# Moving the result transposes, the PSUM banks and the weight conversions in an attention + two-MLP kernel

## The chip, the cores and the metric

The kernel runs on one core of a Trainium2 chip. The metric is the device time of one execution in microseconds (us). Lower is better.

The core has a matrix engine (TensorE; PE in the profile, PEld its weight loads), a vector engine (VectorE; DVE), a scalar or activation engine (ScalarE; ACT), GpSimd (POOL) and a queue engine that here only issues transfers (SyncE; SP). Each runs its instructions in their order in its own stream, and waits on semaphores for the others. PSUM, the memory that TensorE writes to, has eight banks, and a bank holds one 128 x 512 float tile.

## The reference, cut to what matters

```python
k_all = concat([k_g, k_l]); v_all = concat([v_g, v_l])
out_g = softmax(scale * q_g @ k_all.T) @ v_all          # 32 global queries per head see all 544 keys
s_ll = where(|i - j| <= 32, scale * q_l @ k_l.T, -1e9)  # 512 local queries per head see a band
s_lg = scale * q_l @ k_g.T                              # and the 32 global keys
out_l = softmax(concat([s_lg, s_ll])) @ v_all
x = concat([out_g, out_l]) as (2176, 512) tokens        # 4 batches, 8 heads, head size 64
h = x @ w_in;  x2 = max(0.01 * h, h) @ w_out            # 512 -> 2048 -> 512
h = x2 @ w_in2;  out = (h - tanh(h)) @ w_out2           # 512 -> 2048 -> 512
```

The four weight matrices come as 64-bit floats; all else is 32-bit. The MLP products are each made as three products of split operands (high x high, low x high, high x low).

## The kernel before, in words

**Attention stages.** `stage(s)` (L889) holds one pair of heads and one half (256 queries) of a batch: 32 stages, two halves to a pair of heads, eight stages to a batch. A stage is a list of operations that the caller puts between other work:

- `keys` (odd stages): `k_prep` and `q_prep` transpose the next pair's keys and queries through PSUM, and `k_glob` adds the global keys.
- the scores: `score` (L452) makes 32 small products into two banks (`sps`), `smax_a` (L471) takes the minimum and the exponentials. From stage 10 on, four DVE instructions add the mask, reduce, and are the only readers of the two score banks.
- `cols` (L895): `av(s - 2)` multiplies the probabilities of two stages earlier by the values into a bank `avps`, and DVE divides by the sums (`av_out`, tile `o`); `g_score(s)` makes the global queries' scores into the same bank; `copy_v` has POOL rearrange values (`vx`). `g_run` calls what is due of the global part: `g_min`, `g_exp`, `g_norm`, `g_trans` (five transposes into the banks of tags `gtps` and `gt2ps`), `g_av` (40 products into `gavps`), and then `load_v`.
- `turns` (L947): `p_trans(s - 1)` (L495) transposes the probabilities of the stage before (`ptps`, copied out by ACT as `pt`).

`o_trans(pp, tag)` (L537) transposes a stage's result `o` into a bank `otps`; ACT copies it out rounded (`xh`), and DVE subtracts that from the bank (`xl`): the two halves of the MLP's input. Only after `xl` is the bank free. In stages 3 to 9 `o_trans(s - 3)` stands in `turns`; stage 9 has a second one, of stage 7's result, into the bank of tag `avps`. From stage 11 on it is called by `score_op` (L930), right before the scores of stage s:

```python
if s > PRE and s - 1 not in ends:
    o_trans(s - 3, tag("otps"))
score(s, [tag("sps0"), tag("sps1")])
smax_a(s)
```

and `score_op` and `cols` are one operation there (L942).

**Banks.** In stages 0 to 9 each kind of tile has a bank of its own (`start_tags`, L874). Afterwards the attention has three (`run_tags`, L878), given out in turn by `tag` (L882): a tile takes the bank of the third request before it. The bank `h` and the four banks `y0` to `y3` belong to the MLPs by then.

**MLP items.** An item (phase, c, f) is block f of 16 of the hidden layer for a chunk c of tokens (`sizes`: 512, 512, 512, 256 and 384). `mlp1_a` makes twelve matmuls into the bank `h` in four steps, and ACT's activation `g` empties it; `mlp1_b`, two items later, makes twelve into the y banks in four steps. The order of items (L1058) makes stretches: items 0 to 7 are chunk 0 with the first half of f, 8 to 23 chunk 1, 24 to 31 chunk 0 with the second half of f, 32 to 47 chunk 2, 48 to 63 chunk 3, 64 to 79 chunk 4; then the second MLP. Stages 0 to 9 run ahead of item 0; stages 10 to 17 are spread between the steps of items 0 to 7, 18 to 25 between those of items 24 to 31, and the rest beside items 32 to 47 (`beside`, L1065 to L1079). Each such run of stages ends with the transpose of its last result.

**Conversions.** A weight block of 64-bit floats (512 KB) is loaded into one of two buffers (`wraw`, issued by SP) and converted: `rebias` on ACT, then `first`, `second`, `third` on DVE (`convert_parts`, L140); after `third` the buffer is free, and `job` (L828) issues the load of the job after next into it. Blocks of the first output matrix are then split into `woh` and `wol`, used and stored; blocks of the second MLP's matrices (`w2f`) are only stored, for later. `job_at[n]` (L989 to L1009) says how many jobs run beside item n: the first at its start, a second at its middle. Before: items 1 to 8, 11 to 13, 15 and 16 one each, 17 to 22 two each, 23 and 24 one, 35 to 47 one or two (17 jobs), 49, 51, 53 and 55 one. `y_part` (L252) loads a partial sum back into the same two buffers, at items 27 and 29; it is added at the end of item 33.

**What sets the order.** PE's order up to item 77 is the program's (`manual_schedule`, L978 to L984). Those of ACT, DVE and SP are the program's until stage 9 is through (`InTurn`, L21); after that a scheduler places them by its own timeline. `behind` keeps conversions back behind the latest attention and MLP instructions issued by then.

Of the kernel before, what the change touches and what calls it, by code (L numbers as in the profile page):

```python
# [37 lines left out]
def kernel(  # L38
# [28 lines left out]
    PRE, SKEW = 10, 2  # L67
# [174 lines left out]
    HF = NF // 2  # L242
# [189 lines left out]
    def k_glob(j):  # L432
        b, p = divmod(j, NP)
        to = k_t[j][:, :640].rearrange("p (k n) -> p k n", k=5)
        vector.tensor_copy(to[:, :, 96:], kgt[b % 2][:, p : p + 1].to_broadcast([128, 5, SG]))
# [433 lines left out]
    def g_run(n):  # L869
# [3 lines left out]

    start_tags = {  # L874
        "kps": "h", "qps": "att0", "sps0": "att1", "sps1": "y0", "avps": "att2", "sgps": "y1", "ptps": "y2", "otps": "y3",
        "qgps": "h", "gavps": "att2", "gtps": "att0", "gt2ps": "h",
    }
    run_tags = ["att0", "att1", "att2"]  # L878
    ntag = [0]
# [2 lines left out]
    def tag(kind):  # L882
        if tags[0] is start_tags:
            return start_tags[kind]
        t = tags[0][ntag[0] % len(tags[0])]
        ntag[0] += 1
        return t

    def stage(s):  # L889


        ops, late = [], []
        last = NU // 2 - 1

        def cols():  # L895
            ps = bank(tag("avps"), "avps")
            outs = []
            if s >= 2:
                outs.append(av(s - 2, ps))
            if s <= last:  # L900
                outs.append(g_score(s, ps[:, 4 * (D + 1) :] if s >= PRE else bank(tag("sgps"), "sgps")))
            if s < PRE:
                late.append(outs.pop())
            for o in outs:
                o()
            if s >= 1:
                copy_v(s - 1)
            if s <= last and s % 4 == 3:
                j = s // 2
                b, quad = j // NP, j % NP // 2  # L910
                gtodo.extend([
                    (2 * s + 1, lambda: g_min(b, quad)),
                    (2 * s + 2, lambda: g_exp(b, quad)),
                    (2 * s + 3, lambda: g_norm(b, quad)),
                    (2 * s + 5, lambda: g_trans(b, quad, [tag("gtps"), tag("gt2ps")])),
                    (2 * s + 7, lambda: (g_av(b, quad, tag("gavps")), load_v(2 * b + quad + 2))),
                ])
                gtodo.sort(key=lambda x: x[0])
            g_run(2 * s)

        def keys():
            j = (s + 1) // 2
            k_prep(j, tag("kps"))
            k_glob(j)
            q_prep(j, tag("qps"))
            load_kq(j + 2)

        if s % 2 and s + 1 <= last:
            ops.append(keys)
        def score_op():  # L930
            if s > PRE and s - 1 not in ends:
                o_trans(s - 3, tag("otps"))
            score(s, [tag("sps0"), tag("sps1")])
            smax_a(s)

        if s <= last:
            ops.append(score_op)
        else:
            ops.append(lambda: s - 1 in ends or o_trans(s - 3, tag("otps")))
        ops.append(cols)  # L940
        if s >= PRE and s <= last:
            cols_op, first_op = ops.pop(), ops.pop()  # L942
            ops.append(lambda: (first_op(), cols_op()))

        def turns():  # L947
            if 1 <= s <= last + 1:
                p_trans(s - 1, tag("ptps"))
            if 3 <= s < PRE:  # L950
                o_trans(s - 3, tag("otps"))
            if s == PRE - 1:
                o_trans(s - 2, tag("avps"))
            while late:
                late.pop()()
            if s % (2 * NP) == 3 and s // (2 * NP) + 1 < B:
                qg_prep(s // (2 * NP) + 1, tag("qgps"))
            g_run(2 * s + 1)
            if s % (2 * NP) == 1 and s // (2 * NP) + 1 < B:
                qg_load(s // (2 * NP) + 1)  # L960

        ops.append(turns)
        return ops

    ends = (17, 25)
# [23 lines left out]
    job_at, due = {}, 0.0  # L989
# [2 lines left out]
    REST = 2 * NF + 2  # L992
    for n in range(4 * NF - 3):
        out_f = 1 <= n <= HF or 2 * HF < n <= 3 * HF
        early = 11 <= n < 23 and n != 14
        if n > REST:
            due += 7.2 if n < 3 * NF else 2.9
        job_at[n] = int(out_f) + int(early) + int(due / 5.5)
        due %= 5.5
        if out_f:  # L1000
            jobs.append(("out", w1_out, o_todo.pop(0)))
        for _ in range(job_at[n] - int(out_f)):
            if w2_todo:
                jobs.append(w2_todo.pop(0))
            else:
                job_at[n] -= 1
        if n == 3 * HF:
            jobs.extend([None] * 2)
    assert not w2_todo and not o_todo  # L1009

    if True:
# [10 lines left out]
        load_v(0)  # L1022
        in_load()
        k_prep(0, tag("kps"))
        q_prep(0, tag("qps"))
        qg_prep(0, tag("qgps"))
        k_glob(0)
        load_kq(2)
        parts, lows = [], []
        for pp in range(PRE):  # L1030
# [36 lines left out]
        for last, n0, n1 in ((17, 0, HF), (25, 3 * HF, 4 * HF), (NU // 2 + 1, 2 * NF, 3 * NF)):  # L1067
            ops = []
# [28 lines left out]
        for n in range(len(items) + 8):  # L1097
            ph, c, f = items[n] if n < len(items) else (3, 0, 0)
            one = items[n - 1] if 0 < n <= len(items) else (3, 0, 0)
            if ph == 1:  # L1100
                if n in (0, 2, 4, 6) or HF <= n < 2 * HF:
                    in_job()
                if n in (0, 2, 3) or 4 <= n < 12:
                    with tc.issue_after(last_kq[0].ins):
                        in_load()
                if n == REST:
                    job_load()
                    job_load()
                jobs_now = job_at.get(n, 0)
                if jobs_now:  # L1110
                    job()
                if n in (3 * HF + 3, 3 * HF + 5):
                    y_part((n - 3 * HF - 3) // 2)
                if c == 4 and f == 0:
                    while gtodo:
                        gtodo.pop(0)[1]()
                    assert not raws and not jobs
                    att_ctx.close()
                    p2 = ctx.enter_context(tc.tile_pool(name="p2", bufs=1))
                    for k in range(NF - 1):  # L1120
                        wo2_t.append([p2.tile([128, ND, 128], F32R, name=f"wo2{x}{k}") for x in "hl"])
                    wo2_t.append([x[0][:, :, 512:] for x in (xh, xl)])
                    x2_load(0, 0)
                    x2_load(0, 1)
                if c == 4:
                    w2_fetched = [fetch2(w2o_dram[f], False), fetch2(w2i_dram[f], f >= 3 + ND)]
                    if 3 <= f < 3 + ND:
                        x2_split(0, f - 3)
            elif ph == 2 and order2.index(c) + 1 < 5:
                nx = order2[order2.index(c) + 1]  # L1130
                if f in (2, 3):
                    x2_load(nx, f - 2)
                if 5 <= f < 5 + ND:
                    x2_split(nx, f - 5)
            if n in fetch_at:
                fetches.extend(items1[m][2] for m in fetch_at[n])
            while fetches:
                wo_fetch(fetches.pop(0))
            ops = beside.pop(n, [])
            if ph == 2:  # L1140
                mlp2_a(c, f)
            if ph == 3:
                while p_t:
                    mlp2_split()
            steps, last = [], []
            for k in b_at.get(n, []):
                p, c1, f1 = items[k]
                if p == 1:
                    steps += mlp1_b(c1, f1)
                else:  # L1150
                    last.append((c1, f1))
            if ph == 1:
                steps = mlp1_a(c, f) + steps
            if ph == 1 and not ops and gtodo:
                ops = [gtodo.pop(0)[1]]
            K, M = len(ops), len(steps)
            at = [int((i + 0.5) * M / K) for i in range(K)]
            for m, step in enumerate(steps):
                if ph == 1 and jobs_now > 1 and m == M // 2:
                    job()  # L1160
                step()
                while at and at[0] <= m:
                    at.pop(0)
                    ops.pop(0)()
            for op in ops:
                op()
            for c1, f1 in last:
                mlp2_b(c1, f1)
            if ph == 1 and c == 4:
                for kind, t in zip(("out", "in"), w2_fetched):  # L1170
                    behind(lambda: w2_place(kind, f, t))
            fix(n + 1)
            stores()
# [30 lines left out]
```

## Time and profile before

| | |
|---|---|
| median of 3 runs | 917.63 us (916.68 to 918.47) |
| the profiled execution | 917.32 us, of which the span of its instructions is 915.4 us |
| PE busy | 877.8 us (96% of the span) |
| DVE busy | 612.1 us (67%) |
| ACT busy | 505.3 us (55%) |
| POOL busy | 124.2 us (14%) |
| chain that ended last | PE 83%, DVE 7%, DMA 4%, ACT 4% |

Times in the profile are microseconds from the first instruction. "A <- B" behind a wait says that B ended it. A name such as `avps` is a tile, L72 the helper that issues all matmuls, L30 the helper through which ACT, DVE and SP are called. PEclk is the clock that TensorE was granted, as a share of 2.4 GHz; it has two levels, 1.0 and 0.5, so a mean between them tells for what part of a stretch it was at the lower. Busy times of a pipelined engine overlap, so a group of matmuls is best read by its first start and the next group's.

### The profile page before, as it was taken

How to read it: one execution, taken by the hardware profiler on the slowest of the kernel's cores; microseconds unless marked ns; L12 is line 12 of the kernel's file. 1: busy time of each engine (PE TensorE's matmuls, PEld its weight loads, DVE VectorE, ACT ScalarE, POOL GpSimd, SP SyncE). 2: the span in 40 equal slices, each digit the busy share in tenths (PEclk: the TensorE clock that was granted, in tenths of full speed). 3: DMA queues.
4: the chain of work that ended last, by engine and by line, in shares of the span. 5: the costliest groups of instructions: out<-in, count | busy, mean ns of one | idle time of the engine just before them, and what ended most of it. 6: DMA issues, size and time to landing. Idle time of an engine off the chain costs nothing.

```text
span 915.4 us, 18283 instructions
## 1 busy us (share of the span) xinstructions
PE 877.8 (96%) x6908; PEld 743.6 (81%) x6908; DVE 612.1 (67%) x1363; ACT 505.3 (55%) x1053; POOL 124.2 (14%) x247
## 2 busy tenths in 40 slices
PE   7889899998999999999999999999999999999998
PEld 5667778886777877789999998888888888899997
DVE  4667767766624356554323468888878888888886
ACT  5767665444655355434334566565556555655564
POOL 5654420000423132100000000000000000000022
PEclk9989999999999999999999999999999999999999
DMA  9658779678655476679966752001000100010010
GB/s 202 151 151 244 209 217 270 206 221 247 204 135 133 120 219 202 206 227 298 328 202 198 245 196 81 1 18 63 1 1 24 46 1 1 1 47 1 0 36 23
DMA packets 120167, 123.08 MB, mean 134 GB/s; under 512 B 62736, under 2 KB 82448, under 8 KB 120080
## 3 DMA queue, kind: packets, MB, share of 16 engines
q1 hardware_dynamic: 117552, 121.21, 44.2%
q10 hardware_dynamic: 2528, 0.72, 0.4%
q8 instruction: 54, 0.88, 0.4%
q14 instruction: 33, 0.27, 0.1%
HBM read 95.16 MB, written 26.74 MB: 133 GB/s over the span
## 4 chain that ended last, share of the span: by engine, by line
PE 83%; DVE 7%; DMA 4%; ACT 4%; issue 1%; ACTq 0%; SPq 0%; DVEq 0%
PE h L72 38%; PE o L72 20%; PE y L72 17%; DMA wraw<-in_moe_w_out_dram 3%; PE avps L72 2%; DVE wt L30 2%; PE gavps L72 1%; DVE wf L30 1%; DVE xl L30 1%; PE ptps L499 1%; ACT e L30 1%; DVE gl L30 1%; PE qps L441 1%; DMA yraw<-yd 1%; PE sps L72 1%
## 5 line engine op out<-in xcount | busy, mean ns | idle before, releaser
L72 PE MATMUL h<-xh,win 128*128 128x512 f32 (+2 forms) x1280 | 356.4, 362 | 6.2 <-ACT g L30 5.3
L72 PEld LDWEIGHTS h<-xh,win 128*128 128x128 f32 x1280 | 231.5, 190 | 41.5 <-ACT g L30 7.2
L72 PE MATMUL h<-xl,win 128*128 128x512 f32 (+2 forms) x640 | 230.4, 360 | 0.0
L391 POOL COPY vx<-vr 32x260 f32<-32x260 f32 (+3 forms) x208 | 101.1, 486 | 260.1 <-issue 142.9
L72 PEld LDWEIGHTS h<-xl,win 128*128 128x128 f32 x640 | 121.5, 190 | 15.6
L30 DVE TENSOR_TENSOR gl<-g,gh 128x512 fp32r<-128x512 f32 (+2 forms) x80 | 50.0, 626 | 119.8 <-ACT gh L30 119.6
L72 PE MATMUL y<-gh,woh 128*128 128x512 f32 (+2 forms) x320 | 118.8, 371 | 0.0
L72 PE MATMUL y<-gh,wol 128*128 128x512 f32 (+2 forms) x320 | 114.7, 358 | 1.0 <-DMA wol<-wod 1.0
L72 PE MATMUL y<-gl,woh 128*128 128x512 f32 (+2 forms) x320 | 114.3, 359 | 0.0
L72 PE MATMUL o<-wo2l,gh 128*128 128x512 f32 x255 | 99.6, 391 | 0.0
L72 PE MATMUL o<-wo2h,gh 128*128 128x512 f32 x255 | 99.4, 390 | 0.0
L72 PE MATMUL o<-wo2h,gl 128*128 128x512 f32 x255 | 97.4, 390 | 0.0
L30 ACT ACTIVATE g<-h 128x512 f32<-128x512 f32 (+2 forms) x80 | 42.6, 533 | 97.7 <-PE h L72 97.0
L30 ACT ACTIVATE u<-h 128x512 f32<-128x512 f32 (+2 forms) x80 | 42.6, 533 | 89.0 <-PE h L72 81.3
L721 POOL TENSOR_TENSOR gl<-p,gh 128x256 fp32r<-128x256 f32 x16 | 11.8, 740 | 518.8 <-ACT gh L30 516.9
L30 ACT ACTIVATE gh<-p 128x512 fp32r<-128x512 f32 (+2 forms) x80 | 45.5, 568 | 41.9 <-DVE p L30 41.8
L72 PEld LDWEIGHTS y<-gh,woh 128*128 128x128 f32 x320 | 60.5, 189 | 8.0
L72 PEld LDWEIGHTS y<-gl,woh 128*128 128x128 f32 x320 | 60.3, 188 | 8.0
L72 PEld LDWEIGHTS y<-gh,wol 128*128 128x128 f32 x320 | 60.6, 189 | 7.6 <-DMA wol<-wod 1.4
L30 ACT ACTIVATE u<-u,consts 128x512 f32<-128x512 f32 (+2 forms) x80 | 52.7, 658 | 6.8 <-DVE p L30 4.1
L721 DVE TENSOR_TENSOR gl<-p,gh 128x512 fp32r<-128x512 f32 (+1 forms) x64 | 41.9, 654 | 21.4 <-ACT gh L30 21.3
L72 PEld LDWEIGHTS o<-wo2h,gl 128*128 128x128 f32 x255 | 47.9, 188 | 10.1
(116 smaller groups left out, 1361.1 us busy)
## 6 DMA issues: line engine op xcount, KB each, us to landing
wraw<-in_moe_w_out_dram SPq DMA_DIRECT2D x32, 512.0 KB, 4.7
woh<-wod SPq DMA_DIRECT2D x64, 256.0 KB, 4.1
wol<-wod SPq DMA_DIRECT2D x64, 256.0 KB, 3.4
inraw<-in_moe_w_in_dram SPq DMA_DIRECT2D x16, 512.0 KB, 5.6
wraw<-in_moe_w_in_dram SPq DMA_DIRECT2D x16, 512.0 KB, 5.0
wod<-woh SPq DMA_DIRECT2D x16, 256.0 KB, 4.8
wod<-wol SPq DMA_DIRECT2D x16, 256.0 KB, 4.7
w2id<-w2f SPq DMA_DIRECT2D x16, 256.0 KB, 5.2
```

Source lines behind the costliest of these rows:

```text
L30: got = getattr(self.engine, name)(*args, **kwargs)
L72: nc.tensor.matmul(o, lhsT, rhs, start=start, stop=stop, skip_group_check=shared)
L391: last_cp.append(nc.gpsimd.tensor_copy(to, src))
L441: nc.tensor.transpose(ps[:, 128 * t : 128 * t + 128], qr[:, t].rearrange("p h d -> p (h d)"), ident)
L499: nc.tensor.transpose(ps[:, k * 128 : k * 128 + 128], e[:, k // 2, k % 2], ident)
L721: eng["pool" if i == order2[-1] else "dve"].tensor_sub(gl[:, :N], p, f32(gh)[:, :N])
```

## The change

- From stage 11 on, `o_trans(s - 3)` moves out of the operation that begins with the scores, to `turns`, right behind `p_trans(s - 1)`. It is the same stage's later operation, with MLP steps between. As the requests for banks now come in another order, so do the banks.
- Stage 7's result is transposed in item 0, ahead of its third step (of four), and no longer at the end of stage 9.
- Stages 0 to 9: `gavps` goes to the bank `att0` and not `att2`; `gt2ps` to `y2` (that of `ptps`) and not `h`; the first `g_av`, with the `load_v` behind it, comes one operation later (in `cols` of stage 7, not `turns` of stage 6).
- At the very start `qg_prep(0)` and `k_glob(0)` come ahead of `q_prep(0)`, with the bank of `otps` in place of `h`.
- Conversions: items 17, 19 and 21 have one job and not two; items 25 to 30, which had none, have one each; items 35 to 47 have one each (13 jobs and not 17); then 49, 52, 54, 57 and 59. `y_part` issues both its loads at item 31.

```diff
--- before.py
+++ after.py
@@ -873,7 +873,7 @@
 
     start_tags = {
         "kps": "h", "qps": "att0", "sps0": "att1", "sps1": "y0", "avps": "att2", "sgps": "y1", "ptps": "y2", "otps": "y3",
-        "qgps": "h", "gavps": "att2", "gtps": "att0", "gt2ps": "h",
+        "qgps": "h", "gavps": "att0", "gtps": "att0", "gt2ps": "y2",
     }
     run_tags = ["att0", "att1", "att2"]
     ntag = [0]
@@ -913,7 +913,7 @@
                     (2 * s + 2, lambda: g_exp(b, quad)),
                     (2 * s + 3, lambda: g_norm(b, quad)),
                     (2 * s + 5, lambda: g_trans(b, quad, [tag("gtps"), tag("gt2ps")])),
-                    (2 * s + 7, lambda: (g_av(b, quad, tag("gavps")), load_v(2 * b + quad + 2))),
+                    (2 * s + (7 if s > PRE - 4 else 8), lambda: (g_av(b, quad, tag("gavps")), load_v(2 * b + quad + 2))),
                 ])
                 gtodo.sort(key=lambda x: x[0])
             g_run(2 * s)
@@ -927,20 +927,12 @@
 
         if s % 2 and s + 1 <= last:
             ops.append(keys)
-        def score_op():
-            if s > PRE and s - 1 not in ends:
-                o_trans(s - 3, tag("otps"))
-            score(s, [tag("sps0"), tag("sps1")])
-            smax_a(s)
-
         if s <= last:
-            ops.append(score_op)
-        else:
-            ops.append(lambda: s - 1 in ends or o_trans(s - 3, tag("otps")))
+            ops.append(lambda: (score(s, [tag("sps0"), tag("sps1")]), smax_a(s)))
         ops.append(cols)
         if s >= PRE and s <= last:
-            cols_op, first_op = ops.pop(), ops.pop()
-            ops.append(lambda: (first_op(), cols_op()))
+            cols_op, score_op = ops.pop(), ops.pop()
+            ops.append(lambda: (score_op(), cols_op()))
 
 
 
@@ -949,8 +941,8 @@
                 p_trans(s - 1, tag("ptps"))
             if 3 <= s < PRE:
                 o_trans(s - 3, tag("otps"))
-            if s == PRE - 1:
-                o_trans(s - 2, tag("avps"))
+            if s > PRE and s - 1 not in ends:
+                o_trans(s - 3, tag("otps"))
             while late:
                 late.pop()()
             if s % (2 * NP) == 3 and s // (2 * NP) + 1 < B:
@@ -992,11 +984,11 @@
     REST = 2 * NF + 2
     for n in range(4 * NF - 3):
         out_f = 1 <= n <= HF or 2 * HF < n <= 3 * HF
-        early = 11 <= n < 23 and n != 14
+        early = n in (11, 12, 13, 15, 16, 18, 20, 22) or 3 * HF < n < 4 * HF - 1
         if n > REST:
             due += 7.2 if n < 3 * NF else 2.9
-        job_at[n] = int(out_f) + int(early) + int(due / 5.5)
-        due %= 5.5
+        job_at[n] = int(out_f) + int(early) + int(due / 7.1)
+        due %= 7.1
         if out_f:
             jobs.append(("out", w1_out, o_todo.pop(0)))
         for _ in range(job_at[n] - int(out_f)):
@@ -1004,7 +996,7 @@
                 jobs.append(w2_todo.pop(0))
             else:
                 job_at[n] -= 1
-        if n == 3 * HF:
+        if n == 4 * HF - 2:
             jobs.extend([None] * 2)
     assert not w2_todo and not o_todo
 
@@ -1022,9 +1014,9 @@
         load_v(0)
         in_load()
         k_prep(0, tag("kps"))
+        qg_prep(0, tag("otps"))
+        k_glob(0)
         q_prep(0, tag("qps"))
-        qg_prep(0, tag("qgps"))
-        k_glob(0)
         load_kq(2)
         parts, lows = [], []
         for pp in range(PRE):
@@ -1109,8 +1101,9 @@
                 jobs_now = job_at.get(n, 0)
                 if jobs_now:
                     job()
-                if n in (3 * HF + 3, 3 * HF + 5):
-                    y_part((n - 3 * HF - 3) // 2)
+                if n == 4 * HF - 1:
+                    y_part(0)
+                    y_part(1)
                 if c == 4 and f == 0:
                     while gtodo:
                         gtodo.pop(0)[1]()
@@ -1156,6 +1149,8 @@
             K, M = len(ops), len(steps)
             at = [int((i + 0.5) * M / K) for i in range(K)]
             for m, step in enumerate(steps):
+                if n == 0 and m == 2:
+                    o_trans(PRE - 3, tag("otps"))
                 if ph == 1 and jobs_now > 1 and m == M // 2:
                     job()
                 step()
```

## Rows read from the trace of the kernel before

**Rows 1.** The page: the span, and busy time, share and instructions of each engine.

```profile
span 915.4 us, 18283 instructions
PE 877.8 (96%) x6908; PEld 743.6 (81%) x6908; DVE 612.1 (67%) x1363; ACT 505.3 (55%) x1053; POOL 124.2 (14%) x247
```

**Rows 2.** PE's waits, whole span: what waited, for what; us in total, times, longest.

```profile
PE avps L72 <- DVE xl L30: 12.3, 19, 1.9
...
PE gavps L72 <- DVE o L30: 2.3, 1, 2.3
...
PE otps L542 <- DVE o L30: 1.7, 1, 1.7
...
PE h L72 <- ACT pg L30: 0.8, 1, 0.8
```

**Rows 3.** Stretches: us; busy PE, PEld, DVE, ACT, POOL (instructions); PEclk, DMA share, GB/s.

```profile
36.00:43.00 7.00, 5.65 (x130) 5.12 (x130) 3.40 (x12) 2.90 (x9) 1.21 (x4) 0.76 0.28 64
54.00:63.00 9.00, 8.16 (x98) 5.86 (x96) 5.64 (x19) 4.89 (x14) 3.92 (x9) 0.62 0.34 120
62.00:133.00 71.00, 64.40 (x882) 51.10 (x881) 48.95 (x151) 49.97 (x118) 28.88 (x52) 0.98 0.72 201
115.00:121.00 6.00, 4.99 (x58) 4.00 (x58) 4.09 (x17) 2.77 (x8) 2.75 (x6) 0.72 0.42 134
...
214.00:220.00 6.00, 5.89 (x19) 4.68 (x20) 4.52 (x8) 2.12 (x5) 0.00 (x0) 0.72 0.82 255
238.00:310.00 72.00, 68.58 (x955) 54.84 (x955) 28.69 (x125) 40.53 (x102) 23.57 (x54) 1.00 0.46 128
```

**Rows 4.** Timeline, one stage beside items 0 to 7: start, us, instruction [idle before].

```profile
113.13 0.38 PE L542 MATMUL otps<-ident,o 128*128 128x128 f32 x2
...
113.44 0.67 PE L72 MATMUL sps<-kt,qt 64*32 64x128 f32 x32
...
116.01 0.25 PE L72 MATMUL avps<-vr,pt 128*32 128x65 f32 x2 [1.91 <-DVE xl L30]
...
117.53 0.28 DVE L30 CUSTOM_DVE_ANT_0 e<-sps,mask 128x128 f32<-128x128 f32 x1
```

**Rows 5.** PE's waits from 190 to 330 us, the same columns as in rows 2.

```profile
PE h L72 <- ACT g L30: 4.3, 3, 2.2
```

**Rows 6.** Pieces of the chain that ended last: start, us, what.

```profile
7.73 0.63 PE qgps L564 x4
...
37.35 2.01 PE gavps L72 x40
...
175.81 2.72 PE y L72 x12
...
198.41 0.67 ACT wf L30
...
200.29 0.70 DVE wf L30
...
201.05 3.91 DMA wraw<-in_moe_w_out_dram
...
204.99 0.67 ACT wf L30
```

**Rows 7.** Timeline of ACT behind the first `g_av`.

```profile
39.40 0.22 ACT L30 ACTIVATE xh<-gavps 128x64 fp32r<-128x64 f32 x1 [2.21 <-PE gavps L72]
```

**Rows 8.** Timeline from stage 9 to item 0.

```profile
52.69 0.61 ACT L30 ACTIVATE pt<-ptps 128x512 f32<-128x512 f32 x1
...
53.72 0.41 PE L542 MATMUL otps<-ident,o 128*128 128x128 f32 x2 [1.73 <-DVE o L30]
...
55.51 1.22 PE L72 MATMUL h<-xh,win 128*128 128x512 f32 x2 [0.84 <-ACT pg L30]
```

**Rows 9.** Groups: one POOL copy, 55 to 133 us (first) and 235 to 310: busy, mean ns.

```profile
L391 POOL COPY vx<-vr 32x260 f32<-32x260 f32 x21 | 10.5, 501 | 1.0
...
L391 POOL COPY vx<-vr 32x260 f32<-32x260 f32 x21 | 8.7, 415 | 1.0
```

## The prediction

> **What bounds the kernel now.** First the page: PE is busy for 96% of the span and no other engine for more than 67% [rows 1]. So a gain must come from PE's idle time, or from its clock. Second, PE's waits. The reader should see that one wait outweighs the rest: `avps` waits 19 times for `xl`, 12.3 us in all, 1.9 at the longest; three single waits of the first stages stand beside it, 2.3, 1.7 and 0.8 us [rows 2]. Third, the stretches with the granted clock. There are four short ones in which the mean falls to 0.62 to 0.76, each right at or behind a wait: 36 to 43, 54 to 63, 115 to 121 and 214 to 220 us. At the lower level (1.2 GHz) PE does half as much, so what is lost is stretch x (1 - clock): 7 x 0.24 = 1.7, 9 x 0.38 = 3.4, 6 x 0.28 = 1.7 and 1.7 us [rows 3].
>
> Fourth, one stage in order of time, for the cause of the big wait. The result's transposes start at 113.13, the scores at 113.44, and the next tile, `avps`, at 116.01 after 1.91 us of idle, ended by `xl` [rows 4]. The code says why: the requests are `otps`, `sps0`, `sps1`, `avps`, the fourth takes the first one's bank, and all four stand in one operation. Only 0.67 us of scores lie between the transposes and the tile that needs their bank back.
>
> **The change part by part.**
>
> *The transposes behind the probabilities.* The order becomes `sps0`, `sps1`, `avps`, `ptps`, `otps`. `avps` still takes the bank of the `otps` before it in stages without keys, but now a gap of MLP steps and the scores lie between; in the others it takes that of `qps`. In the first run of stages 21 operations share items of eight steps, three operations to an item, so a gap is two or three steps of three matmuls, 3 x 2.72 / 12 = 0.68 us each [rows 6]: 1.4 us or more. That covers the longest wait but for 0.5 us, with the scores still in between, so the 12.3 us go. What is late next: `otps` takes the bank of `sps1`, whose last reader is the fourth of DVE's mask instructions. In the worst stage the scores end at 113.44 + 0.67 = 114.11 and that reader at 117.53 + 0.28 = 117.81 [rows 4], 3.7 us later. The transposes come behind `av` and `g_score` (28 small products, an estimate of 0.7 us by the 32 of the scores in 0.67), a gap of 1.4 and the four transposes of `p_trans` (0.6, by four others that take 0.63 [rows 6]): 2.7 us. So 1.0 us of the worst wait comes back. Bounds: nothing comes back (gain 12.3), or half does (6). I take 10.8, that is 1.5 returned, as most of the 19 waits are far below the longest. The low clock at 115 to 121 follows on the longest wait and should go with it: 1.7, bounds 0 and 1.7.
>
> *Stage 7's result in item 0.* Removed: the waits of 1.73 and 0.84 us ahead of the first `h` matmul [rows 8]; with the bank `h` free of `gt2ps`, the second has no cause left. Added: `gt2ps` now needs the bank of `ptps`, and ACT's copy of that ends at 52.69 + 0.61 = 53.30 [rows 8], about 0.7 us after PE could be there; and in item 0 the third step's 0.7 us must cover ACT's and DVE's halves of the new transposes before the fourth step reads them, which I put 0.7 us short (ACT has the exponentials in front). Net 2.6 - 1.4 = 1.1. Bounds: 2.6 if both are covered, -1 if DVE's conversions get in front. The low clock at 54 to 63 (3.4 us) has lost its largest wait, but the stretch keeps waits; I take half, 1.7, bounds 0 and 3.4.
>
> *The first `g_av` one operation later.* Its wait of 2.3 us [rows 2] goes, as `att0` has long been free, and its 40 products, 2.01 us at the low clock [rows 6], cost about 1.0 at full. But PE is not alone in setting the pace there: ACT sat idle for 2.21 us behind it [rows 7], and that is about what the next stage can come forward; beyond it ACT and DVE are the chain. I take 2.0, bounds 0.5 and 3.5 (wait and clock, 4.0, less the rest). `load_v` comes with it, later by one operation; POOL's copies for stage 8 cover it, and if they ran out it would cost POOL about 1 us, and PE nothing until `av(8)`, two stages on.
>
> *The start.* The global queries' transposes (0.63 us on the chain [rows 6]) go where PE waits for the queries' load. 0.5; bounds 0 and 0.63.
>
> *Conversions.* A buffer's turn is load plus conversion: from one `rebias` to the next 204.99 - 198.41 = 6.6 us, of which 200.29 + 0.70 - 198.41 = 2.6 convert and 3.9 load [rows 6]. With two jobs to an item, each buffer must turn once in 2 x 2.72 = 5.4 us and can't; ACT waits for the load with `g` behind it, and the `h` matmuls wait 4.3 us in three waits [rows 5], with 1.7 us of clock behind them [rows 3]. Three jobs in two items need a turn every 7.3 us, which fits. I leave 1.0 us of the 6.0: gain 5.0, bounds 2 and 6. By the Trainium skill (DMA: Bandwidth & Descriptors, Anatomy of one DMA), a load takes 2.0 us plus its bytes at 436 GB/s; 512 KB would be 3.2 us, an estimate, and nothing of the 6.0 would be left. The trace's 3.9 decides.
>
> The six jobs that move to items 25 to 30 find room: in 238 to 310 us DVE is busy for 28.7 and ACT for 40.5 of 72 us, the DMA share is 0.46 [rows 3], and six conversions are 6 x (2.6 - 0.67) = 11.6 us of DVE. But POOL's copies of values run there too. The same copy takes 501 ns beside conversions and 415 without [rows 9], so POOL's 23.6 us [rows 3] would become some 28 of 72: hidden, 0 us on the path. The Trainium skill (SBUF — State Buffer, Who interferes with whom) has it harsher: a DVE instruction with two SBUF inputs blocks POOL's reads altogether while it runs. If all 11.6 us of conversion blocked POOL it would be busy for 35 of 72, still no bound; the rows show far less. Chunk 2's thinning and the one job more in chunk 3 stand at 0 (bounds -1 and 1). `y_part` comes up to four items later; two full items of some 9 us (72 / 8) still lie ahead of its use, and if the load came late the end of item 33 would wait for it.
>
> *Sum.* 10.8 + 1.7 + 1.1 + 1.7 + 2.0 + 0.5 + 5.0 = 22.8 us. From 62 to 133 us DVE and ACT are busy for 49 and 50 of 71 us [rows 3]; with the stretch about 8 us shorter that is near 80%, so I allow 2.0 us of new waits for them. Gain 20.8. The profiled execution took 917.3 us (span 915.4 and 1.9 around it), 0.3 us under the median: 917.3 - 20.8 = 896.5.
>
> **The rivals.** (1) *The wait moves to `otps`.* The three bank rotation stays, and the transposes now wait for the slowest readers. For: the 3.7 us above. Against: only the worst stage is so late. Half of the 12.3 us returns, and the clock with it: 10.8 + 1.7 shrinks to 6, so 903. (2) *The conversions stay too dense.* Turns of 7.3 us wanted against 6.6 and more needed leave little; a load of 5 us instead of 3.9 makes a turn 7.7. Then 4 of the 5.0 us stay: 900.5. (3) *Slower.* The same place as (1), but DVE is late everywhere: 21 transposes wait for their score readers. The sum is used up from 20.8 / 21 = 1.0 us of wait at each, that is readers done 2.7 + 1.0 = 3.7 us after the scores as a mean; at 2 us of wait each, 42 in all, the time is about 939. DVE would have to be late on average as in the worst stage shown, for the point alone. (4) *The change doesn't do what it says.* From stage 10 on, DVE, ACT and SP are ordered by a scheduler with a timeline of its own; it could put conversions ahead of `xl` and `g` so that each gain is lost again: about 917.
>
> **How the numbers follow.** About 0.2% (1.8 us) is what a measurement of this kernel can tell from no change. Forecast 0.66, its own range 890 to 902 by the bounds of its terms (all the best ends would give 887); rival 1 0.13, rival 2 0.10, rival 3 0.06, rival 4 0.05. Range 888 to 906: it takes in rivals 1 and 2 and leaves out 3 and 4 and some of the tails. Faster: 0.66 + 0.13 + 0.10 and a fifth of rival 4, 0.90; same 0.04; slower 0.06.
>
> **What would show it.** Right: no `avps` wait for `xl` in PE's waits; `otps` waits for DVE of at most 2 us together; no `h` wait for `g` over 1 us between 190 and 240 us; clock 1.00 through 115 to 121 and 214 to 220; `gavps` without a wait and the first `h` matmul 3 to 5 us sooner; items 24 to 31 no longer than before, with longer POOL copies. Wrong: `otps` waiting in most stages (1 or 3); ACT waiting for `wraw` with `g` behind it (2); low clock at new places; a new wait of `y` for `wol` or of DVE for `y_part`, if the queue order breaks.

## The result, and the profile after

The changed kernel takes 902.16 us (median of 4 runs, 900.66 to 903.52), the kernel before 917.15 on the same chip: ratio 0.9834, 95% interval 0.9813 to 0.9855. That is 15.0 us less. The range held it (888 to 906), the direction was right, and the forecast of 896.5 was 5.7 us too low.

The page of the changed kernel answers to [rows 1]:

```profile
span 900.7 us, 18292 instructions
PE 872.7 (97%) x6908; PEld 740.3 (82%) x6908; DVE 612.7 (68%) x1363; ACT 502.6 (56%) x1053; POOL 124.1 (14%) x247
```

PE's waits over the whole span answer to [rows 2] and [rows 5] (what waited, for what; us in total, times, longest):

```profile
PE gt2ps L634 <- ACT pt L30: 5.2, 4, 1.6
PE kps L425 <- DMA kr<-in_k_l_dram: 4.4, 1, 4.4
PE qgps L564 <- ACT sg L30: 2.5, 1, 2.5
PE kps L425 <- ACT sg L30: 2.4, 1, 2.4
...
PE h L72 <- ACT g L30: 1.1, 2, 0.7
PE h L72 <- DVE xl L30: 1.0, 1, 1.0
PE gavps L72 <- ACT sg L30: 1.0, 1, 1.0
PE otps L542 <- DVE st L30: 0.9, 1, 0.9
...
PE h L72 <- ACT xh L30: 0.8, 1, 0.8
```

The 12.3 us of `avps` for `xl` are gone to the last wait, and so are the three waits of `h` for `g` beside items 21 to 24 (4.3 us) and those of `gavps` and `otps` for `o`. What stands there now is new: `gt2ps`, `qgps`, `kps` and `gavps` wait for copies of ACT, `pt` and `sg`, and item 0 waits for its own transposes (0.9, 0.8 and 1.0).

The stretches, with the columns of [rows 3]:

```profile
36.00:43.00 7.00, 7.00 (x207) 6.00 (x195) 5.29 (x17) 5.58 (x17) 5.15 (x9) 1.00 0.62 138
54.00:66.00 12.00, 10.72 (x67) 8.46 (x67) 5.33 (x12) 4.92 (x11) 1.10 (x2) 0.57 0.41 97
62.00:133.00 71.00, 63.04 (x835) 49.36 (x835) 47.70 (x149) 47.23 (x111) 25.96 (x48) 0.95 0.73 203
75.00:79.00 4.00, 3.50 (x18) 2.42 (x26) 3.22 (x8) 1.82 (x6) 1.30 (x2) 0.57 0.92 249
115.00:121.00 6.00, 3.55 (x23) 2.78 (x22) 5.93 (x16) 4.79 (x13) 1.96 (x4) 1.00 0.22 33
...
214.00:220.00 6.00, 6.00 (x28) 4.99 (x27) 3.62 (x6) 2.46 (x4) 0.00 (x0) 1.00 0.80 228
238.00:310.00 72.00, 71.64 (x914) 57.83 (x914) 36.00 (x130) 38.55 (x95) 21.89 (x46) 1.00 0.64 178
```

The stretch from 238 to 310 us has 71.6 us of PE where it had 68.6, with the moved conversions in DVE's column (36.0 for 28.7). From 62 to 133 us PE is busy for less than before, though the `avps` waits are gone there too. The low clock is now at 54 to 66 and 75 to 79 us and costs 12 x 0.43 + 4 x 0.43 = 6.9 us; before it cost 1.7 + 3.4 + 1.7 + 1.7 = 8.5.

Where the time went is read from the start of each chunk's first `h` matmul, in us. The columns are one execution each, and those of single parts belong to the experiments below:

| item | before | after | transposes only | conversions only | start only | after, item 0 undone |
|---|---|---|---|---|---|---|
| 0 | 55.51 | 48.32 | 56.88 | 52.73 | 50.78 | 49.92 |
| 8 | 133.32 | 131.96 | 137.60 | 129.88 | 127.69 | 130.86 |
| 24 | 228.56 | 220.52 | 232.68 | 218.46 | 224.26 | 219.41 |
| 32 | 302.51 | 291.85 | 303.70 | 291.82 | 299.38 | 290.20 |
| 48 | 416.04 | 402.57 | 413.82 | 405.33 | 412.89 | 400.91 |
| 64 | 468.24 | 453.55 | 464.75 | 456.65 | 464.40 | 452.70 |

Item 0 starts 7.2 us sooner, and item 8 only 1.4: items 0 to 7 became 5.8 us longer (83.6 for 77.8) and gave most of the start back. PE's waits in them are 10.6 us where they were 6.4, and the mean clock is 0.92 for 0.94, which is 2.0 us more of low clock. Items 8 to 23 gained 6.7, 24 to 31 gained 2.6, chunk 2 2.8 and chunk 3 1.2.

### The profile page after: what moved, and what is told of

It reads as the page before. It is cut to its first block, busy times and chain, and to the rows that moved or that the text cites. A ratio compares the mean times of both kernels' runs of the same rounds, so it can differ in the third digit from the quotient of the medians.

```text
span 900.7 us, 18292 instructions
## 1 busy us (share of the span) xinstructions
PE 872.7 (97%) x6908; PEld 740.3 (82%) x6908; DVE 612.7 (68%) x1363; ACT 502.6 (56%) x1053; POOL 124.1 (14%) x247
## 4 chain that ended last, share of the span: by engine, by line
PE 87%; DVE 5%; ACT 4%; DMA 2%; issue 1%; ACTq 0%; SPq 0%; DVEq 0%
PE h L72 39%; PE o L72 21%; PE y L72 19%; PE sps L72 2%; PE avps L72 2%; PE gavps L72 1%; ACT e L30 1%; DMA yraw<-yd 1%; DVE wt L30 1%; PE ptps L499 1%; PE qps L441 1%; PE kps L425 1%; DVE e L30 1%; DMA wod<-woh 1%; DVE wf L30 1%
```

## The experiments

All ratios are to the kernel before on the same chip, with their 95% intervals.

**The parts alone.** Four kernels, run together. The first has only the transposes behind the probabilities (stage 7's second transpose stays in stage 9):

```diff
-            if s > PRE and s - 1 not in ends:
-                o_trans(s - 3, tag("otps"))
             score(s, [tag("sps0"), tag("sps1")])
...
+            if s > PRE and s - 1 not in ends:
+                o_trans(s - 3, tag("otps"))
```

> Only the result transposes move behind the probabilities; all else as before. Theory T (the new order of requests puts kps, qgps and the global transposes behind the bank of avps or ptps, whose ACT copies are late while weights are converted): the 19 avps waits for xl go everywhere, but in items 0 to 7 waits of 3 to 6 us for ACT's sg and pt take their place, so that stretch keeps its length and only items 24 to 47 gain their 6 us: about 911 us. Rival V (the give-back comes from stage 7's transposes in item 0 and the low clock behind them, which this kernel does not have): the whole 12.3 us and the clock at 115 us are gained: about 903 us.

Measured: 913.06 us, ratio 0.9947 (0.9928 to 0.9967): 4.9 us less by the ratio, 4.1 by the medians. Its PE waits from 60 to 137 us, and the wait that stood there in the kernel before (second):

```profile
PE qgps L564 <- ACT sg L30: 2.5, 1, 2.5
PE kps L425 <- ACT sg L30: 2.5, 1, 2.5
PE gt2ps L634 <- ACT pt L30: 1.2, 1, 1.2
PE h L72 <- ACT g L30: 1.1, 1, 1.1
PE gavps L72 <- ACT sg L30: 1.0, 1, 1.0
```

```profile
PE avps L72 <- DVE xl L30: 5.7, 7, 1.9
```

No `avps` wait for `xl` is left, and 7.2 us of waits of `qgps`, `kps`, `gt2ps` and `gavps` are there in place of 5.7, more than T's 3 to 6. Items 0 to 7 take 80.7 us for 77.8, so the part loses 2.9 us there, and gains from item 24 on (from 1.2 us late at item 32 to 2.2 early at item 48). Transposes in item 0, theory V, aren't needed for the give-back; the low clock comes without them too (a mean of 0.92 in these items).

The second has only the conversions and the loads of the partial sum (`job_at`, `y_part`):

> Only the conversions and the loads of the partial sum move; all else as before. T and V alike: h no longer waits for g in items 21 to 24, the lower clock behind it goes, items 17 to 24 gain 6 to 7 us, chunk 3 another 1 us: about 910 us. Rival W (the conversions beside items 24 to 31 lengthen those, hidden in the changed kernel by the transposes' gain): items 24 to 31 get longer by over 1 us, 912 us or more.

Measured: 907.94 us, ratio 0.9900 (0.9867 to 0.9933): 9.2 us less. Between items 8 and 32 it gains 7.3 us, and items 24 to 31 take 73.4 us where they took 73.9 without conversions. W falls. Some 2.8 us more are gained before item 0, where nothing was edited; that is the clock (below).

The third has only the start:

> Only the start changes: global queries first, the first global value product one operation later and in another bank, gt2ps with ptps; items as before. The first h matmul should come 5 to 7 us sooner (7.2 in the changed kernel, of which stage 7's second transpose, still here, takes some 1 to 2). Theory T: PE sets the pace of items 0 to 7, so most of it is kept at item 8, 5 us: about 912 us. Rival U (in items 0 to 7 the conversions on DVE and ACT set the pace, and what comes sooner waits later): under 2 us are left at item 8: about 916 us.

Measured: 912.28 us, ratio 0.9950 (0.9935 to 0.9965). Item 0 starts 4.7 us sooner and item 8 5.6: PE, not DVE and ACT, paces items 0 to 7 as long as the old order stands, as T has it. But 2.5 us of it are lost from item 8 to item 32, where this kernel still has two conversions to an item: `h` waits 6.7 us for `g` there, and before it was 4.3.

The fourth is the changed kernel with stage 7's transposes at the end of stage 9, as before:

```diff
+            if s == PRE - 1:
+                o_trans(s - 2, tag("avps"))
...
-                if n == 0 and m == 2:
-                    o_trans(PRE - 3, tag("otps"))
```

> The changed kernel with stage 7's result transposed at the end of stage 9 as before, not in item 0. Rival V: the waits of 0.9, 0.8 and 1.0 us in item 0 go and with them most of the 10 us of low clock from 55 to 65 us; up to 1.7 us come back ahead of item 0: 898 us. Theory T: the low clock stays, since it comes with the small matmuls of the stages beside items 0 and 1, and the ACT waits at 75 and 120 us stay: 901 to 903 us.

Measured: 901.34 us, ratio 0.9822 (0.9798 to 0.9845); the changed kernel's is 0.9834. Item 0 starts 1.6 us later and item 8 1.1 sooner. The move to item 0 is worth nothing that can be measured, and V falls: without it items 0 to 7 still take 80.9 us, at a mean clock of 0.94. Whether the small matmuls bring the low clock, as T says, no run here shows.

By their ratios the three parts alone add up to 18.7 us (4.9, 9.2 and 4.6), and the whole gains 15.2. Their intervals reach 1.8, 3.0 and 1.4 us to either side, so this does not show that one part costs another something.

**Bank order or conversions?** T says that the tiles behind `otps` got a bad bank. From the trace of the changed kernel, the wait of `qgps` (start, us, instruction [idle before]):

```profile
72.20 0.60 PE L499 MATMUL ptps<-ident,e 128*128 128x128 f32 x4
...
73.07 0.58 ACT L30 ACTIVATE pt<-ptps 128x512 f32<-128x512 f32 x1
...
73.32 0.88 DVE L30 SCALAR_TENSOR_TENSOR wf<-wraw,wt 128x512 int32<-128x512 int32 x1
...
74.13 0.41 DVE L30 TENSOR_TENSOR o<-avps,sum 128x256 f32<-128x256 f32 x1
...
74.24 0.63 ACT L30 ACTIVATE woh<-wf 128x512 fp32r<-128x512 f32 x1 [0.32 <-DVE wf L30]
...
74.89 0.55 ACT L30 ACTIVATE sg<-avps 64x128 f32<-64x128 f32 x2
...
75.50 0.69 PE L564 MATMUL qgps<-ident,qgr 64*128 64x64 f32 x4 [2.48 <-ACT sg L30]
```

`qgps` is the third request after `avps` now, so it needs that bank; before, it needed that of `sps1`. The bank is free when ACT has copied the global scores `sg` out of it, and ACT, which works in order, first makes `woh`, which waits for DVE's conversion `wf`. But that is the smaller part: the bank's other reader, DVE's `o`, stands behind the same conversion and ends at 74.54, and in no stage beside items 0 to 7 and 24 to 31 does `sg` start before `o` has ended. So `woh` holds `sg` for 0.3 us here, and DVE's order, with conversions ahead of `o`, for most of the rest. The next kernel changes the order of requests and leaves the load: where the next stage begins with keys, the result's transposes come behind its queries, so `kps` has the bank of `sps1` again.

```diff
-            if s > PRE and s - 1 not in ends:
+            if s > PRE and s - 1 not in ends and (s % 2 or s + 2 > last):
                 o_trans(s - 3, tag("otps"))
...
             q_prep(j, tag("qps"))
+            if s - 1 > PRE and s - 2 not in ends:
+                o_trans(s - 4, tag("otps"))
```

> The changed kernel, but where the next stage begins with the keys, the result's transposes come behind that stage's query transposes, so that kps takes the bank of sps1, and no longer that of avps. Theory T (bank order): the 2.45 us wait of kps for ACT's sg at 120 us and the 1.0 us wait of gavps shrink by 2 us or more together, the 2.5 us of qgps stay; items 0 to 7 get 2 to 4 us shorter: 898 to 900 us. Rival U (conversions on DVE and ACT set the pace there): the same time is waited at qps, otps or ptps instead, item 8 starts within 1 us of the changed kernel's: 902 us.

Measured: 903.63 us, ratio 0.9853 (0.9838 to 0.9867). Its PE waits from 60 to 137 us:

```profile
PE qgps L564 <- ACT sg L30: 2.5, 1, 2.5
PE gt2ps L634 <- ACT pt L30: 2.0, 1, 2.0
PE qps L441 <- ACT sg L30: 2.0, 1, 2.0
PE h L72 <- ACT g L30: 0.7, 1, 0.7
```

`kps` no longer waits; `qps`, one request later, does, and `gt2ps` waits longer. Item 8 starts at 132.3 for 132.0. Between these two orders the banks only choose which tile waits (6.5 us of such waits for 7.2): U. With item 0 undone as well:

> Both the keys' order of the run before and stage 7's result transposed at the end of stage 9. T: the gains add: 896 to 899 us. U: no better than the kernel with item 0 alone undone: 901 us.

Measured: 900.96 us, ratio 0.9826 (0.9809 to 0.9842), no better than item 0 undone alone (0.9822). U again.

The load is tried by taking it away. This kernel leaves out the three DVE conversion instructions of the first eight output blocks, so that those weights are not converted:

```diff
+        parts = parts[:n]
...
-            wo_split(f, converted(raw))
+            wo_split(f, converted(raw, n=1 if f < HF else 4))
```

> The changed kernel without the three DVE instructions of the conversions of the first eight output blocks (items 1 to 8): that part of the weights is not converted, 8 x 1.9 = 15 us of DVE less. If ACT's late copies come from ACT waiting for conversions on DVE (both T and U): the waits of qgps, kps, gavps and gt2ps beside items 0 to 7, 7.2 us together, fall under 3 us, and item 8 starts 4 to 7 us sooner: about 896 us. If the bank order alone makes them, whatever DVE does: they stay over 5 us and the time at 901 us or more.

Measured: 898.14 us, ratio 0.9792 (0.9770 to 0.9815). Its PE waits from 60 to 133 us:

```profile
PE gt2ps L634 <- ACT pt L30: 1.4, 2, 1.2
PE qgps L564 <- DMA inraw<-in_moe_w_in_dram: 1.1, 1, 1.1
PE qps L441 <- ACT pt L30: 1.0, 1, 1.0
PE h L72 <- ACT g L30: 0.7, 1, 0.7
PE gavps L72 <- ACT sg L30: 0.4, 1, 0.4
```

Of the 7.2 us at the four tiles 2.9 are left, just under the 3 us as written, with the banks as in the changed kernel. `qps`, behind `kps`, now waits 1.0: 3.9 in all, so DVE's conversions make about half of these waits. (The wait of `qgps` is put down to a DMA, but ACT's `sg` ended at 70.40 us and `qgps` starts at 70.46.) Item 8 starts at 124.3 for 132.0, more than forecast. Waits make 3.3 of those 7.6; the low clock, which this profile does not show in any stretch of the items, holds much of the rest. That is in part the luck of one execution: of the four runs two have a mean clock of 0.999 and 1.000 (896.4 and 896.6 us), and two of 0.994 and 0.996 (899.8 and 899.7).

**The start's first term.** The kernel before with only the global queries first:

> Before, with only the global queries' transposes ahead of the queries' at the very start. My prediction's term: 0.5 us, at most 0.63. If the start gains more from it, as the changed kernel's trace suggests (its scores of stage 2 start 1.9 us sooner): 1.5 to 2 us at the first h matmul. Time: 915 to 917 us.

Measured: 916.13 us, ratio 0.9997 (0.9980 to 1.0014). Its item 0 starts at 52.53, that of the conversions-only kernel, which has the old start, at 52.73. So 0.2 us, from one execution each, and the 1.9 us that I had read off the changed kernel's trace were not this.

**Relieving ACT.** If ACT stands behind `woh`, another engine can make `woh`. Both kernels build on the one with the keys' order and item 0 undone (900.96). First POOL, for items 1 to 8:

```diff
-        scalar.activation(hi, w, AF.Copy)
+        if pool:
+            nc.gpsimd.tensor_copy(hi, w)
+        else:
+            scalar.activation(hi, w, AF.Copy)
```

> The kernel with the keys' order and item 0 undone, and besides, the rounded copies woh of the first eight output blocks (items 1 to 8) are made by POOL, not by ACT, so that ACT no longer stands waiting for DVE's conversion with sg, pt and g behind it. Theory U, in the form that ACT's order is what makes the waits: those of qgps, qps and gt2ps beside items 0 to 7 (6.5 us together there) fall under 3 us, 897 to 899 us. Rival P (DVE's own load sets the pace, or POOL's copies of values come late behind the new ones): the waits stay over 5 us in all, or avps waits for vx: 901 us or more.

Measured: 904.85 us, ratio 0.9879 (0.9847 to 0.9912), slower than its base. PE's waits from 60 to 137 us:

```profile
PE y L72 <- DVE wol L30: 6.8, 2, 3.9
PE gt2ps L637 <- ACT pt L30: 1.7, 1, 1.7
PE qps L444 <- ACT sg L30: 0.9, 1, 0.9
PE h L72 <- ACT g L30: 0.7, 1, 0.7
```

`woh` now stood behind POOL's copies of values, `wol` came late, and the `y` matmuls waited 6.8 us. The waits for ACT's `sg` and `pt` fell from 6.5 to 2.6 us, as U's form says, but this does not show that it was ACT's order: the 2.5 us of `qgps`, most of the fall, went behind a wait of PE itself, in which ACT and DVE caught up:

```profile
73.11 0.80 PE L72 MATMUL y<-gh,wol 128*128 128x512 f32 x1 [3.95 <-DVE wol L30]
```

With the input blocks' `win` on POOL too:

> As the run before, and the rounded copies win of the four input blocks of items 0, 2, 4 and 6 on POOL too. U: another 0.5 to 1 us less, 896 to 898 us. P: slower than the run before, since POOL, busy for some 29 of the first 71 us of items, takes 12 more copies beside conversions: 901 us or more.

Measured: 904.81 us, ratio 0.9885 (0.9855 to 0.9914): no different, neither U's gain nor P's further loss, and `y` waits 7.5 us. Then DVE itself, in place of POOL:

```diff
-            nc.gpsimd.tensor_copy(hi, w)
+            vector.tensor_copy(hi, w)
```

> As the kernel with the keys' order and item 0 undone, but the rounded copies woh of items 1 to 8 are made by DVE itself, right behind its conversion, not by ACT or POOL. If ACT's order is what makes the waits of qgps, qps and gt2ps (6.5 us there): they fall under 3 us, and with no POOL in between wol is in time: 897 to 900 us. If DVE's load sets the pace: 8 copies of about 0.45 us, 3.6 us of DVE more, make otps, g or y wait instead: 901 to 904 us.

Measured: 897.89 us, ratio 0.9782 (0.9751 to 0.9812): the fastest full kernel here, below the changed one (0.9813 at the least), if by a hair; with its base's interval (from 0.9809) it overlaps by as little. Its PE waits from 60 to 133 us, and those of its base (second):

```profile
PE qgps L567 <- ACT sg L30: 2.2, 1, 2.2
PE qps L444 <- ACT sg L30: 1.8, 1, 1.8
PE gt2ps L637 <- ACT pt L30: 1.6, 1, 1.6
PE h L72 <- ACT g L30: 0.7, 1, 0.7
PE avps L72 <- ACT qgd L30: 0.2, 1, 0.2
PE ptps L502 <- DVE st L30: 0.2, 1, 0.2
```

```profile
PE qgps L564 <- ACT sg L30: 2.5, 1, 2.5
PE gt2ps L634 <- ACT pt L30: 2.0, 1, 2.0
PE qps L441 <- ACT sg L30: 2.0, 1, 2.0
PE h L72 <- ACT g L30: 1.7, 1, 1.7
```

The time is that of ACT's order, but the waits are not: `qgps`, `qps` and `gt2ps` still wait 5.6 us, not under 3, and in all it is 6.7 us for 8.2, so 1.5 us of the 3.1. Another stretch of low clock that the base's profile has at 74 us is missing here, worth 1.7. How much of the gain is the edit stays open. Why the waits stay is in the trace of this run:

```profile
70.80 0.41 DVE L30 TENSOR_TENSOR o<-avps,sum 128x256 f32<-128x256 f32 x1
...
71.24 0.55 ACT L30 ACTIVATE sg<-avps 64x128 f32<-64x128 f32 x2 [0.65 <-DVE o L30]
...
71.85 0.46 PE L567 MATMUL qgps<-ident,qgr 64*128 64x64 f32 x4 [2.19 <-ACT sg L30]
```

With `woh` out of its way ACT is free 0.65 us before `sg`, which waits for DVE's `o`. With `win` on DVE too:

> As the run before, and the rounded copies win of the input blocks of items 0, 2, 4 and 6 on DVE too. ACT's order: another 0.5 us less, 896 to 900 us. DVE's load: slower than the run before by about as much, 902 to 905 us.

Measured: 901.32 us, ratio 0.9821 (0.9792 to 0.9849), between the two forecasts. The gain is gone and `qgps`, `qps` and `gt2ps` wait 6.9 us for 5.6, as with DVE's load. But the profile also loses 5.1 us to the low clock ahead of item 8, and that of the run before 1.7, so how much of ACT's work DVE has room for stays open.

## Why the prediction was right or wrong, point by point

**The transposes: the step that failed.** I wrote "I take 10.8, that is 1.5 returned". The 12.3 us did go, and `otps`, which I had waiting for the score readers, waits only 0.9 us in the whole run, in item 0. But the working followed one tile. Moving one request in a rotation of three banks gives every later tile another predecessor: `qgps`, `kps` and the global tiles now need the banks of `avps` and `ptps`, which ACT must empty, and ACT is late beside conversions: with `sg` mostly because DVE's `o` is late, with `pt` because ACT's own part of a conversion, `rebias`, comes first (two of them, 127.72 to 128.93 us, ahead of the `pt` at 128.84 for which `gt2ps` waits 1.2). Leaving out DVE's conversions took about half of these waits away, so that half is shown by a run and the rest is read from the trace alone. Beside items 0 to 7 the new order returned 2.5 + 2.4 + 1.2 + 1.0 = 7.2 us where 5.7 had been, and `gt2ps` 0.7 in chunk 2. Alone, the part gains 4.9 us, not 10.8 + 1.7. Rival 1 had the size (903) and the wrong tile. The allowance of 2.0 us for DVE and ACT was the right worry, sized too small. That the forecast is only 5.7 us off is in part luck: this term gave too little, and the conversions gave more than their bound.

**Conversions: right, under-sized.** 5.0 us expected, bounds 2 and 6; items 8 to 23 gain 6.7 in the changed kernel, and items 8 to 31 gain 7.3 in the kernel with this part alone. Items 20 to 23 took 28.4 us and now take 21.8, which is four items of 2 x 2.72 with nothing left over: the 1.0 us that I left did not stay. The 3.9 us that I took for a load was the shortest of its stretch (170 to 225 us: 3.9 to 5.5, 4.3 as the median). The changed kernel's loads there take 3.6 to 6.4 us, again 4.3 as the median, so a turn is 2.6 + 4.3 = 6.9 us and fits into 7.3. Rival 2, which needed 5 us, is out. By the Trainium skill's fit of a load's time (DMA: Bandwidth & Descriptors, Anatomy of one DMA), an estimate of 3.2 us, nothing would be left, and nothing is; but the page takes that fit from transfers that GpSimd issues, these are issued by SP, and none of them was as short. No run here timed a load apart from other traffic, so this does not test the fit.

**The fourth stretch: right.** The conversions are hidden. The POOL copy of [rows 9] takes 475 ns beside them (24 copies, from 225 to 300 us), between its 415 and 501. The Trainium skill (SBUF — State Buffer, Who interferes with whom) has the two contend for a port that one of them holds at a time. On average the copies are slowed by a seventh; whether a single one is stopped altogether meanwhile, as I put it, these means do not show.

**The start: right as a sum, on the second look.** Against 7.2 us at item 0, I had 0.5 + 2.0 and, ahead of item 0, 2.6 less 0.7. But 55.51 is one execution of the old start: it has item 0 at 52.73 in the profile of the conversions alone and at 56.88 in that of the transposes alone, by the clock. The full start gives 50.78, 2.0 us less than the first of these, which like it has no low clock ahead of 45 us: near the 0.5 + 2.0 + 0.8 - 0.7 = 2.6 that I had for it. By its ratio the start alone gains 4.6 us; eight of its ten runs have a mean clock of 0.996 and two of the sixteen of the kernel before, so some of it is low clock that the old start has in most runs. `gt2ps` waits 1.6 us, where I had 0.7. Stage 7's move gives 1.6 us at item 0 and costs 2.7 inside items 0 to 7 (83.6 for 80.9 us): nothing, for the 1.1 + 1.7 predicted (2.6 - 1.4 is 1.2, not 1.1).

**The clock: a term that was not one.** I counted 1.7 us at 115 and 1.7 at 54 us, and let 1.7 go with the conversions. The profile lost 8.5 us to the low level before and 6.9 after, so 1.6 came of 5.1. Of my signs of being wrong one came true, low clock at a new place: 75 to 79 us, behind the 2.5 us of `qgps`. The last section says why such terms can't be added up.

**Slower, or no effect (rivals 3 and 4):** neither; `otps` does not wait in the stages.

## What to carry to other kernels

When a request moves in a pool of buffers given out in turn, write down for every tile in the cycle which tile it now follows, who reads that one last, and what that engine has in front; the gain of the moved tile is an upper bound until this is done. A wait for one engine's copy can be another engine's load: here DVE's conversions held `o`, ACT's `sg` came behind it, and the banks waited for `sg`. And price a stretch of low clock from several executions, not from one.

## What the runs showed of the hardware that I had not expected

The granted clock of one kernel is not the same from run to run. Four runs of the conversions-only kernel took 905.73 and 905.29 us at a mean clock of 0.995, and 910.16 and 910.71 at 0.992. The kernel before took 913.95 us at 0.996 and 919.61 us at 0.990 on one chip. The mean clock makes half of the first difference and nearly all of the second: 0.003 of 905 us is 2.7, 0.006 of 917 is 5.5. And the same start, with the same wait of 2.3 to 2.4 us of `gavps`, had the low level in the profile of the kernel before (first) and not in that of the conversions-only kernel (stretches as in [rows 3]):

```profile
36.00:44.00 8.00, 6.65 (x138) 5.96 (x138) 4.33 (x15) 3.88 (x12) 2.15 (x5) 0.79 0.39 84
```

```profile
36.00:44.00 8.00, 7.87 (x223) 6.78 (x224) 5.78 (x16) 4.84 (x14) 3.67 (x6) 1.00 0.54 132
```

That is 8 x 0.21 = 1.7 us of PE, and 2.8 us at item 0. A wait comes before each fall here, but not each such wait is followed by one.
